# A held output turn, one q chunk and six bank choices moved in a fused attention and SwiGLU kernel

## The chip, the cores and the metric

The kernel runs on one core of a Trainium2 chip. The metric is device time in microseconds (us) of that core, as the median of several executions. The span of a profile, from first to last instruction, is about 1.9 us shorter than the time. Engines are written PE (tensor matmul), PEld (tensor weight load), DVE (vector), ACT (scalar), POOL (GpSimd) and SP (the queue that issues DMAs).

## The reference

```python
# x: 2048 x 640; 32 heads of 192; the last 512 keys and values of the cache; FFN width 1536
def _A_ref(x, k_cache, v_cache, wq, wo):
    W = min(4096, max(256, Sk // 4))                      # 512
    q = (x @ wq).reshape(B, Sq, Hq, Dh).transpose(0, 2, 1, 3)
    k, v = k_cache[:, :, Sk - W:, :], v_cache[:, :, Sk - W:, :]
    p = softmax(einsum("bhqd,bhkd->bhqk", q, k) * Dh ** -0.5)
    o = einsum("bhqk,bhkd->bhqd", p, v)
    return o.transpose(0, 2, 1, 3).reshape(B, Sq, Hq * Dh) @ wo
def _B_ref(x, w_gate, w_up, w_down):
    return (silu(x @ w_gate) * (x @ w_up)) @ w_down
xn = layernorm(x)
return x + _A_ref(xn, ...) * silu(_B_ref(xn, ...))
```

## The kernel before

The FFN comes first (to about 168 us). Then come 16 head pairs. A pair has four blocks of 512 rows; index `i` counts them. In each pair the scores of all four blocks are made, with the q of the next block in three chunks between them. Then the contexts (`pv`) of a block are woven with the output projection (`wo`) of the block two before. PSUM, the memory that PE writes its results to, has two pools of two bank pairs each, `sc` and `mm`; a pair is free again when DVE or ACT has read it. Most matmuls run as two row tiles of 64 rows at once. The kernel lets the two tiles write different banks: context and projection are made in two turns that exchange banks, and a small POOL memset orders the turns. The second turn of a block's last output tile is *held*: it is issued later, inside the next block's contexts or, at the end of a pair, after the next pair's first q chunk.

```python
def sc_tile(): return psum.tile([P, 2, 512], f32, name="sc", tag="sc")     # bufs=2
def mm_tile(): return psum.tile([P, 2, 512], f32, name="mm", tag="mm")     # bufs=2

def q_rows(i, j):                       # one chunk of q: 10 matmuls of 512 columns
    ...
    q_ps = mm_tile()
    for c in range(NC):                 # 5
        for h, r in enumerate((lo, hi)):
            nc.tensor.matmul(q_ps[:, h, :], pairs[pr]["wq"][r, c, ...], xnT[r, c, ...], ...)
    nc.vector.reduce_sum(qTs[i][:, j, :], q_ps[:, :, :].rearrange("p h n -> p n h"), axis=AX.X)

def scores(i, kc):                      # 6 matmuls of 512 columns, then the exponential
    sc = mm_tile() if i == NS - 1 and kc < 2 else sc_tile()
    ...
    nc.scalar.activation(p_t[:, :, :], sc[:, :, :], ACT.Exp, scale=scale)

def pv_full(i, q2):                     # contexts of the last two pairs, full rows
    ...
    acc = sc_tile() if alone and q2 and b < 2 else mm_tile()
    ...                                 # 16 matmuls of 193 columns
    divide(i, q2, acc, alone)           # DVE and ACT into O_b (bufs=2), DMA transpose to OT_b

# wo_tile(i, qt): first() makes turn 0 of an output tile, second() turn 1 and the DVE accumulation
def wo_last(b, qt, eng):                # output tile of the last pair
    ...
    sc = None if split else sc_tile()
    ...
    nc.vector.tensor_tensor(s_f[:], sc[:, :, 0:HD], g2[...], ALU.mult)
    eng.tensor_tensor(ob[:], s_f[...], sacc[:, t, :], ALU.add)   # eng: POOL, for two tiles DVE

held = []
def drop():
    while held:
        held.pop()()

def woven(i):
    (a, b), (w, x, y, z) = (pv(i, 0), pv(i, 1)), (wo_tile(i - 2, qt) for qt in range(4))
    for part in (*a[:2], drop, w[0], *b[:2], w[1], x[0], *a[2:], x[1], y[0], *b[2:], y[1], z[0]):
        part()
    held.append(z[1])                   # the last tile's second turn waits for other work

for pr in range(NPAIR):
    for b in range(NB):
        i = pr * NB + b
        for kc in range(KC):
            if kc < 3 and i + 1 < NS:
                q_rows(i + 1, kc)
                drop()
            scores(i, kc)
            ...
    for b in range(NB):
        i = pr * NB + b
        if i < 2:
            two(pv(i, 0), pv(i, 1))     # both contexts of the block, their turns alternating
        elif pr < last - 1:
            woven(i)
        ...                             # key loads for pair pr + 2 after b == 0
i = last * NB
work = [(0, 0), (0, 1), (1, 0), (1, 1), (2, 0)]
for b, q2 in work:
    pv_full(i + b, q2)
...                                     # then wo_last, woven with the other contexts
```

The softmax here doesn't subtract the row's maximum and nothing guards it: scores larger than these inputs give would overflow.

Of the kernel before, what the change touches and what calls it, by code (L numbers as in the profile page):

```python
# [15 lines left out]
def kernel(  # L16
# [26 lines left out]
    NC = D // P  # L43
    T = Sq // P
    NB = Sq // 512
# [25 lines left out]
    def sc_tile():  # L71
        return psum.tile([P, 2, 512], f32, name="sc", tag="sc")

    def mm_tile():
        return psum.tile([P, 2, 512], f32, name="mm", tag="mm")
# [40 lines left out]
    def load_v(pr):  # L116
        for h in range(2):
            nc.sync.dma_start(
                out=V_p[:, :, h, 0:Dh],
                in_=vv[2 * pr + h, k0:Sk, :].rearrange("(p j) d -> p j d", j=KC),  # L120
            )
# [21 lines left out]
    def sum_k(pr, c):  # L143
        d = pairs[pr]
        nc.vector.reduce_sum(d["ssum"][:, c : c + 1], d["KT"][:, c, :], axis=AX.X)
# [267 lines left out]
    NS = NPAIR * NB  # L413
# [4 lines left out]



    def q_rows(i, j):
        pr, b = divmod(i, NB)
        if j == 0:
            qTs[i] = qpool.tile([P, 3, 512], bf, name="qT")
        q_ps = mm_tile()
        for c in range(NC):
            for h, r in enumerate((lo, hi)):
                nc.tensor.matmul(  # L428
                    q_ps[:, h, :], pairs[pr]["wq"][r, c, j * P : (j + 1) * P], xnT[r, c, b * 512 : (b + 1) * 512],
                    start=(c == 0), stop=(c == NC - 1),  # L430
                )
        with nc.allow_low_precision(reason="a sum of two, rounded once, like a copy out of PSUM"):
            nc.vector.reduce_sum(  # L433
                qTs[i][:, j, :], q_ps[:, :, :].rearrange("p h n -> p n h"), axis=AX.X
            )
# [13 lines left out]
    def pv(i, q2):  # L449

        pr, b = divmod(i, NB)
        st = {}

        def part(p):
            if p == 0:
                if q2 == 0:
                    Obs[i] = opool.tile([P, 4, 2, Dh], bf, name="O_b")
                    tag = "OT_l" if late(i) and pr < last else "OT_b"
                    OTs[i] = otpool.tile([P, 12, P], bf, name=tag, tag=tag, bufs=2 if tag == "OT_l" else 3)
                st["alone"] = i < 2 or (pr == last and 2 * b + q2 < 5)  # L460
                st["acc"] = sc_tile() if st["alone"] and q2 and b < 2 else mm_tile()
            acc = st["acc"]
            turn, h = divmod(p, 2)
            for kc in range(KC):
                for n, r in enumerate((lo, hi)):
                    k = n ^ turn
                    qt = 2 * q2 + k
                    m = nc.tensor.matmul(  # L468
                        acc[:, k, h * 256 : h * 256 + Dh + 1],
                        Ps[i][kc][r, h, qt * P : (qt + 1) * P], V_p[r, kc, h, 0 : Dh + 1],  # L470
                        start=(p == 0 and kc == 0), stop=(turn == 1 and kc == KC - 1),
                        skip_group_check=True,
                    )
                    after(m, st)
            if p == 1:
                turned(m, st)
            if p == 3:
                divide(i, q2, acc, st["alone"])

        return [lambda p=p: part(p) for p in range(4)]  # L480
# [25 lines left out]
    def pv_full(i, q2):  # L506

        pr, b = divmod(i, NB)
        if q2 == 0:
            Obs[i] = opool.tile([P, 4, 2, Dh], bf, name="O_b")  # L510
            tag = "OT_l" if late(i) and pr < last else "OT_b"
            OTs[i] = otpool.tile([P, 12, P], bf, name=tag, tag=tag, bufs=2 if tag == "OT_l" else 3)
        O_b, OT_b = Obs[i], OTs[i]
        alone = i < 2 or (pr == last and 2 * b + q2 < 5)
        acc = sc_tile() if alone and q2 and b < 2 else mm_tile()
        for k in range(2):
            qt = 2 * q2 + k
            for h in range(2):
                for kc in range(KC):
                    nc.tensor.matmul(  # L520
                        acc[:, k, h * 256 : h * 256 + Dh + 1],
                        Ps[i][kc][:, h, qt * P : (qt + 1) * P], V_p[:, kc, h, 0 : Dh + 1],
                        start=(kc == 0), stop=(kc == KC - 1),
                    )
        divide(i, q2, acc, alone)
# [6 lines left out]
    def late(i):  # L532
        return i // NB >= NPAIR - 2 and i % NB >= 2

    def wo_mm(ps, i, qt, n, first=True, end=True):
        for j in range(3):
            nc.tensor.matmul(  # L537
                ps, OTs[i][:, 3 * qt + j, :], pairs[i // NB]["wo"][:, j, n * HD : (n + 1) * HD],
                start=(first and j == 0), stop=(end and j == 2),
            )  # L540
# [8 lines left out]
    def turned(m, st):  # L549

        st["turn"] = nc.gpsimd.memset(turn_t[:], 0.0)  # L551
        follows(st["turn"], m)

    def after(m, st):
        if "turn" in st:
            follows(m, st.pop("turn"))
# [61 lines left out]
    def wo_last(b, qt, eng):  # L618
        i, t = last * NB + b, 4 * b + qt
        ob = xrs[t] if b < 2 else finp.tile([P, D], bf, name="ob", bufs=4)  # L620
        s_f = finp.tile([P, 2, HD], f32, name="s_f", bufs=4)
        halves = [slice(n * HD, (n + 1) * HD) for n in range(2)]
        split = b == NB - 1 and qt == 3
        sc = None if split else sc_tile()
        ps = [(mm_tile()[:, 0, :] if split else sc[:, n, :])[:, 0:HD] for n in range(2)]
        for n, cols in enumerate(halves):
            if late(i):
                wo_mm(ps[n], i - NB, qt, n, end=False)
            wo_mm(ps[n], i, qt, n, first=not late(i))
            if split:  # L630
                nc.vector.tensor_tensor(s_f[:, n, :], ps[n], g2[:, t, cols], ALU.mult)
                nc.vector.tensor_tensor(ob[:, cols], s_f[:, n, :], sacc[:, t, cols], ALU.add)
                (nc.scalar if n else nc.sync).dma_start(
                    out=out2[t * P : (t + 1) * P, cols], in_=ob[:, cols]
                )
        if split:
            return
        nc.vector.tensor_tensor(  # L638
            s_f[:], sc[:, :, 0:HD], g2[:, t, :].rearrange("p (n d) -> p n d", n=2), ALU.mult
        )  # L640
        eng.tensor_tensor(ob[:], s_f[:].rearrange("p n d -> p (n d)"), sacc[:, t, :], ALU.add)
        stores.append((t, ob))
# [4 lines left out]
            nc.sync.dma_start(out=out2[t * P : (t + 1) * P, :], in_=ob[:])  # L647

    held = []

    def two(x, y):
        for part in (*x[:2], *y[:2], *x[2:], *y[2:]):
# [5 lines that stand above are left out]
# [9 lines left out]
    for pr in range(NPAIR):  # L667
        for b in range(NB):
            i = pr * NB + b
            for kc in range(KC):  # L670
                if kc < 3 and i + 1 < NS:
                    q_rows(i + 1, kc)
                    drop()
                scores(i, kc)
                if pr < last:
                    if b == 0:
                        transpose_k(pr + 1, kc)
                    elif b == 2 and kc < 3:
                        sum_k(pr + 1, kc)
                    elif b == 3:  # L680
                        centre_k(pr + 1, kc)
                        if kc == 3:
                            centre_k(pr + 1, 4)
            if b == 0:
                load_v(pr)
                if pr >= last - 1:
                    for t in range(8):
                        load_xr(t + 8 if pr < last else t)
                        if pr == last:
                            add_x(t)  # L690
        if pr == last:
            break
        for b in range(NB):
            i = pr * NB + b
            if i < 2:
                two(pv(i, 0), pv(i, 1))
            elif pr < last - 1:
                woven(i)
            else:
                for q2 in range(2):  # L700
                    pv_full(i, q2)
                    wo_full(i - 2, 2 * q2)
                    wo_full(i - 2, 2 * q2 + 1)
            if b == 0 and pr + 2 < NPAIR:
                load_k(pr + 2)
            elif b == 1 and pr + 2 < NPAIR:
                load_wq(pr + 2)
            elif b == 2:
                load_wo(pr + 1)
    i = last * NB  # L710
    V, G = nc.vector, nc.gpsimd
# [3 lines that stand above are left out]
# [39 lines left out]
```

## Time and profile before

| | before |
|---|---|
| median of the first 3 runs | 927.31 us (926.93 to 928.28) |
| span of the profile | 925.4 us, granted clock 0.999 |
| PE drawn busy | 917.3 us (99%) |
| next engine, DVE | 575.6 us (62%) |

With PE at 99%, the useful question is where it still stands. "Excess" below means how much later a matmul starts than the regular spacing of matmul starts allows, read from the trace; the prediction gives the spacings and shows the lines. The profile's own views show most of the same waits as idle time of PEld.

### The profile page before, as it was taken

Reading aid. Unit: us, or ns where it says so; the run is one execution under the profiler, and the core shown is the slowest. Engines: PE = TensorE matmul, PEld = TensorE weight load, DVE = VectorE, ACT = ScalarE, POOL = GpSimd, SP = SyncE. Lnnn points to the kernel's source line nnn. Section 1 sums busy time; section 2 is a strip of 40 time slices with the busy share of each in tenths; the row PEclk is TensorE's granted clock in tenths of the full one; section 3 lists DMA queues with packets and bytes.
Section 4 is the critical chain, followed back from the end, with each engine's and each line's share of the span. In section 5 each row is a group of like instructions: output and inputs, shape, how many; then the busy total and the mean of one; then the engine's idle time right before and its main releaser. Section 6 shows DMA issues by size and latency. Waiting matters only on the chain.

```text
span 925.4 us, 25770 instructions
## 1 busy us (share of the span) xinstructions
PE 917.3 (99%) x11085; PEld 624.9 (68%) x11101; DVE 575.6 (62%) x844; ACT 473.8 (51%) x847; POOL 100.1 (11%) x387
## 2 busy tenths in 40 slices
PE   9999999999999999999999999999999999999997
PEld 5455556575858585868686867676767777776665
DVE  6433331467676767676766667676767676767655
ACT  4222222556464646565555565656555555556561
POOL 0000000000000000000000000000000000002976
PEclk9999999999999999999999999999999999999999
DMA  9321510044544445444536262536362717162624
GB/s 298 72 56 33 114 35 1 1 77 89 87 79 83 83 80 86 75 90 70 95 60 106 59 107 55 111 53 113 46 119 42 124 36 129 36 129 76 135 57 140
DMA packets 243810, 77.18 MB, mean 83 GB/s; under 512 B 224624, under 2 KB 243696, under 8 KB 243696
## 3 DMA queue, kind: packets, MB, share of 16 engines
q1 hardware_dynamic: 242640, 74.72, 41.5%
q8 instruction: 87, 1.43, 0.7%
q10 hardware_dynamic: 1056, 0.82, 0.3%
q14 instruction: 27, 0.22, 0.1%
HBM read 39.45 MB, written 2.62 MB: 45 GB/s over the span
## 4 chain that ended last, share of the span: by engine, by line
PE 98%; DMA 1%; DVE 0%; issue 0%; ACT 0%; DVEq 0%
PE mm L428 22%; PE sc L563 19%; PE sc L442 18%; PE mm L468 16%; PE sc L276 11%; PE mm L298 6%; PE sc L537 3%; PE mm L520 2%; DMA wg_sb<-in_B_w_gate_dram 1%; PE mm L276 0%; PE mm L311 0%; DMA OT_b<-O_b 0%; PE sc L520 0%; DMA x_t<-in_A_x_dram 0%; DVE s_f L638 0%
## 5 line engine op out<-in xcount | busy, mean ns | idle before, releaser
L446 ACT ACTIVATE p_t<-sc 128x1024 bf16<-128x1024 f32 x254 | 253.0, 1022 | 130.5 <-PE sc L442 130.5
L433 DVE TENSOR_REDUCE qT<-mm 128x512 bf16<-128x1024 f32 x189 | 231.2, 1223 | 104.8 <-PE mm L428 102.4
L498 ACT ACTIVATE O_b<-mm,r 128x192 bf16<-128x192 f32 x486 | 164.6, 421 | 183.1 <-issue 159.9
L428 PE MATMUL mm<-xnT,wq_p 64*128 64x512 bf16 x1890 | 237.7, 377 | 0.0
L563 PE MATMUL sc<-wo_p,OT_b 64*128 64x320 bf16 x2592 | 217.4, 296 | 0.5 <-DMA OT_b<-O_b 0.5
L588 DVE TENSOR_TENSOR sacc<-sacc,sc 128x640 f32<-128x640 f32 x200 | 164.1, 821 | 78.3 <-PE sc L563 78.3
L442 PE MATMUL sc<-qT,khat 64*128 64x512 bf16 x1524 | 198.3, 377 | 0.0
L468 PE MATMUL mm<-V_p,p_t 64*128 64x193 bf16 x3520 | 186.4, 243 | 0.0
L468 PEld LDWEIGHTS <-p_t 64*128 64x128 bf16 x3584 | 162.6, 94 | 12.0
L428 PEld LDWEIGHTS <-wq_p 64*128 64x128 bf16 x1890 | 105.6, 94 | 96.0 <-issue 0.5
L563 PEld LDWEIGHTS <-OT_b 64*128 64x128 bf16 x2592 | 139.9, 94 | 22.7 <-DMA OT_b<-O_b 1.1
L442 PEld LDWEIGHTS <-khat 64*128 64x128 bf16 x1536 | 85.6, 94 | 79.2 <-issue 2.9
L551 POOL MEMSET turn_t<- 128x1 f32 x328 | 32.2, 98 | 697.9 <-PE mm L468 474.6
L284 DVE TENSOR_TENSOR hT<-sc,sg 128x512 bf16<-128x512 f32 x46 | 31.7, 690 | 85.2 <-ACT sg L283 85.1
L283 ACT ACTIVATE sg<-sc 128x512 bf16<-128x512 f32 x46 | 27.3, 596 | 72.4 <-PE sc L276 72.4
L276 PE MATMUL sc<-xnT,wg_sb 128*128 128x512 bf16 (+1 forms) x248 | 58.6, 354 | 1.0 <-DMA wg_sb<-in_B_w_gate_dram 0.4
L276 PE MATMUL sc<-xnT,wu_sb 128*128 128x512 bf16 (+1 forms) x259 | 59.1, 355 | 0.1
L298 PE MATMUL mm<-wd_sb,hT 128*128 128x320 bf16 x384 | 56.6, 300 | 0.0
L487 DVE RECIPROCAL r<-mm 128x4 f32<-128x4 f32 x124 | 22.7, 183 | 48.1 <-PE mm L468 36.3
L298 PEld LDWEIGHTS <-hT 128*128 128x128 bf16 x384 | 37.5, 98 | 18.9
L276 PEld LDWEIGHTS <-wu_sb 128*128 128x128 bf16 x285 | 26.3, 98 | 26.9
L276 PEld LDWEIGHTS <-wg_sb 128*128 128x128 bf16 x285 | 26.3, 98 | 23.5 <-DMA wg_sb<-in_B_w_gate_dram 0.5
(67 smaller groups left out, 373.1 us busy)
## 6 DMA issues: line engine op xcount, KB each, us to landing
wo_p<-in_A_wo_dram SPq DMA_DIRECT2D x16, 480.0 KB, 4.6
K_p<-in_A_k_cache_dram SPq DMA_DIRECT2D x32, 192.0 KB, 3.4
V_p<-in_A_v_cache_dram SPq DMA_DIRECT2D x32, 192.0 KB, 3.0
wq_p<-in_A_wq_dram SPq DMA_DIRECT2D x64, 80.0 KB, 3.1
wq_p<-in_A_wq_dram SPq DMA_DIRECT2D x16, 160.0 KB, 3.5
x_r<-in_A_x_dram SPq DMA_DIRECT2D x16, 160.0 KB, 3.9
x_t<-in_A_x_dram SPq DMA_DIRECT2D x14, 160.0 KB, 3.0
OT_b<-O_b SPq DMA_TRANSPOSE x124, 2.8
```

The costliest lines, as they stand in the source:

```text
L276: nc.tensor.matmul(out, w_sb[:, c, f * P : (f + 1) * P], xnT[:, c, qc], start=(c == 0), stop=(c == NC - 1),)
L284: nc.vector.tensor_tensor(hTs[b][:, f, :], u, sg[:], ALU.mult)
L298: nc.tensor.matmul(dn[:, 0:HD], hTs[b][:, f, ti * P : (ti + 1) * P], wd_sb[:, f, cols], start=(f == 0), stop=(f == NF - 1),)
L428: nc.tensor.matmul(q_ps[:, h, :], pairs[pr]["wq"][r, c, j * P : (j + 1) * P], xnT[r, c, b * 512 : (b + 1) * 512], start=(c == 0), stop=(c ...
L433: nc.vector.reduce_sum(qTs[i][:, j, :], q_ps[:, :, :].rearrange("p h n -> p n h"), axis=AX.X)
L442: nc.tensor.matmul(sc[:, h, :], khat[r, j, ks], qT[r, j, :], start=(j == 0), stop=(j == 2))
L446: nc.scalar.activation(p_t[:, :, :], sc[:, :, :], ACT.Exp, scale=scale)
L468: m = nc.tensor.matmul(acc[:, k, h * 256 : h * 256 + Dh + 1], Ps[i][kc][r, h, qt * P : (qt + 1) * P], V_p[r, kc, h, 0 : Dh + 1], start=(p ...
L498: nc.scalar.activation(O_b[:, qt, h, :], a_k[:, h, 0:Dh], ACT.Copy, scale=r[:, k, h, :])
L551: st["turn"] = nc.gpsimd.memset(turn_t[:], 0.0)
L563: m = nc.tensor.matmul(ps[:, n, 0:HD], OTs[i][r, 3 * qt + j, :], pairs[i // NB]["wo"][r, j, n * HD : (n + 1) * HD], start=(turn == 0 and j ...
L588: nc.vector.tensor_tensor(s_t, s_t, sc[:, :, 0:HD], ALU.add)
```

## The change

The intent was to remove three kinds of waiting. The held turn goes inside the q chunk, so that DVE frees its bank before it reduces the chunk. One q chunk goes where PE waits for the first transposed contexts. In the last pair other banks are used where one was still being read.

```diff
-    def q_rows(i, j):
+    def q_rows(i, j, between=None):
...
         for c in range(NC):
+            if c == NC - 1 and between:
+                between()
...
-        acc = sc_tile() if alone and q2 and b < 2 else mm_tile()        # pv_full
+        acc = sc_tile() if alone and b == 1 else mm_tile()
...
-        sc = None if split else sc_tile()                               # wo_last
+        sc = None if split else mm_tile() if b >= 2 and qt % 2 == 0 else sc_tile()
...
+    EARLY = (NB + 1, 0)
...
-                if kc < 3 and i + 1 < NS:
-                    q_rows(i + 1, kc)
-                    drop()
+                if kc < 3 and i + 1 < NS and (i + 1, kc) != EARLY:
+                    q_rows(i + 1, kc, drop)
...
                 two(pv(i, 0), pv(i, 1))
+                if i == 1:
+                    q_rows(*EARLY)
```

## The prediction

> **What bounds the kernel now.** I read the page's busy table first, then the chain of waits, then what the tensor engine and its weight loads waited for, and last the timeline around each wait. In the table and the chain the tensor engine (PE) is nearly everything:
>
> ```profile
> PE 917.3 (99%) x11085; PEld 624.9 (68%) x11101; DVE 575.6 (62%) x844; ACT 473.8 (51%) x847; POOL 100.1 (11%) x387
> PE 98%; DMA 1%; DVE 0%; issue 0%; ACT 0%; DVEq 0%
> ```
>
> No other engine passes 62%, so the change, which adds no matmul and removes none, can gain only what PE stands still. "99% busy" does not yet say how little that is: a row-tiled matmul of 512 columns is shown 377 ns long while the next pair starts 216 ns after this one, so a stall of up to about 160 ns hides inside the drawn bar. The waits of the weight loads betray them:
>
> ```profile
> PEld L442 <- issue: 2.9, 14, 0.2
> PEld L520 <- issue: 1.1, 3, 0.4
> PEld L563 <- DMA OT_b<-O_b: 1.1, 2, 0.8
> PEld L537 <- issue: 0.4, 1, 0.4
> ```
>
> Fourteen equal waits before the scores (L442), a few elsewhere. I then took every matmul's start in the trace and subtracted the regular spacing (216 ns a pair for 512 columns, 136 for 320, 83 for 193; unpaired matmuls the same). After 168 us, excess over 25 ns is: fourteen times 88 to 99 ns at the second scores tile of a head pair, 1.26 us together; 0.73 and 0.14 us at the first output projections of the first pair, where the transposed context has not landed; 0.26 and 0.33 us in the last pair; and about 0.1 us at each of four switches between row-tiled and full matmuls, which stay. So some 2.7 us of 927 is in reach, all three parts together.
>
> The fourteen, in the timeline of the pair that starts at 256 us:
>
> ```profile
> 256.25 1.26 PE L428 MATMUL mm<-xnT,wq_p 64*128 64x512 bf16 x10
> 257.33 0.59 PE L563 MATMUL sc<-wo_p,OT_b 64*128 64x320 bf16 x6
> 257.55 1.23 DVE L433 TENSOR_REDUCE qT<-mm 128x512 bf16<-128x1024 f32 x1 [0.67 <-PE mm L428]
> 257.74 0.83 PE L442 MATMUL sc<-qT,khat 64*128 64x512 bf16 x6
> 258.69 0.81 DVE L588 TENSOR_TENSOR sacc<-sacc,sc 128x640 f32<-128x640 f32 x1
> 259.56 0.82 PE L442 MATMUL sc<-qT,khat 64*128 64x512 bf16 x6
> ```
>
> To be seen: q chunk (L428), held second turn of the output projection (L563), first scores, then the second scores at 259.56, which need the bank pair that the held turn filled. It is freed by the accumulation L588, ready at about 257.95 but queued behind the 1.23 us reduction of the q chunk. It ends at 259.505; the scores follow 53 ns later, where the spacing would have let them start at 259.468.
>
> **What the Trainium skill says.** (1) "Perfetto Trace Analysis", Summary: the profiler window per engine type: the end of a TensorE instruction is an estimate, that of a DVE or ACT instruction is observed. Hence starts, not busy time; the 377 against 216 ns agrees. (2) "PSUM — Partial Sum Buffer", Engine vs sequencer instructions: the vector and scalar queues are strict FIFO, and matmuls start and complete in program order. The trace agrees: L588 starts only as L433 ends. (3) "TensorEngine Tiling (Array Packing)", Gotcha 1: different row tiles cannot be in one PSUM bank together. That is why a turn exchanges banks through a small memset (L551). It runs 256.56 to 256.66, long before the held turn at 257.33, so bringing that turn 216 ns forward does not meet it.
>
> **The change part by part.** I also read the two built programs' order on each engine with the semaphores waited on; instruction counts are equal, and only places and banks differ.
>
> *Held turn inside the chunk.* The turn now follows four fifths of the q chunk: it starts at 256.255 + 4 x 0.216 = 257.12, issues for 3 x 0.136 = 0.41, and its last matmul ends near 257.71. L588 goes first on DVE, 257.74 to 258.56, and the reduction after it, 258.48 to 259.70. The second scores find their bank free 0.9 us early. The reduction, now later, holds the bank of the third q chunk, which starts near 260.11: 0.35 us margin. Thirteen pairs gain about 90 ns each: -1.17 us. The fourteenth is pair 1, below.
>
> *The q chunk between contexts (first pair).* Before, PE waits for the first transposes:
>
> ```profile
> 197.25 0.73 ACT L498 ACTIVATE O_b<-mm,r 128x192 bf16<-128x192 f32 x2 [1.26 <-DVE r L487]
> 198.22 0.25 PEld L563 LDWEIGHTS <-OT_b 64*128 64x128 bf16 x6 [0.77 <-DMA OT_b<-O_b]
> 198.22 0.58 PE L563 MATMUL sc<-wo_p,OT_b 64*128 64x320 bf16 x6 [0.55 <-DMA OT_b<-O_b]
> ```
>
> Placed at 196.84, the chunk (5 x 0.216 = 1.08 us) fills that hole: the 0.73 goes, and the later 0.14 with it. But it takes one of the two mm bank pairs. The next context waits for the other until ACT ends at 197.98, so it starts at about 198.03 instead of 197.92: +0.11. The one after it takes the chunk's bank: the reduction runs about 198.14 to 199.36, PE could be there at 198.03 + 0.66 + 0.41 = 199.10 and goes at 199.41: +0.31. Net here -0.45 us.
>
> *What its leaving uncovers (pair 1).* The chunk's old place is empty now, and the held turn falls into the next chunk, after the first scores. In the built order the first scores come directly behind the first turn of the last output tile and wait for DVE: their bank is freed by the accumulation of the tile before. Around 209 us that copy is
>
> ```profile
> 208.95 0.82 DVE L586 COPY sacc<-sc 128x640 f32<-128x640 f32 x1 [0.22 <-PE sc L563]
> 209.15 1.24 PE L428 MATMUL mm<-xnT,wq_p 64*128 64x512 bf16 x10
> ```
>
> It ends at 209.77, so PE, which was free for L428 at 209.147, stands until 209.82: +0.68 us. The second scores then get, in the built order, the bank of the first scores and wait for their exponential, not for the held turn: first scores 209.82, exponential 209.82 + 0.85 + 1.02 = 211.69, PE there at 209.82 + 0.65 + 0.86 + 0.41 + 0.22 = 211.96: no wait. The old 0.10 disappears. Net +0.58 us.
>
> *Banks in the last pair.*
>
> ```profile
> 890.08 1.98 ACT L446 ACTIVATE p_t<-sc 128x1024 bf16<-128x1024 f32 x2
> 891.19 0.99 PE L520 MATMUL sc<-V_p,p_t 128*128 128x193 bf16 x10
> 906.50 1.64 DVE L638 TENSOR_TENSOR s_f<-sc,g 128x640 f32<-128x640 f32 x2 [0.70 <-PE sc L537]
> 907.38 0.57 PE L537 MATMUL sc<-wo_p,OT_l 128*128 128x320 bf16 x3 [0.17 <-DVE s_f L638]
> ```
>
> The second context waited for the exponential of the third scores tile (ends 891.10). It now takes the second tile's bank, whose exponential ends at 890.22, before PE comes (890.91): -0.26. The third and fourth take the banks left, free at 891.10 and 892.06 against PE at 892.24 and 893.57. Its own output's transposes still land at 895.72, before PE at 896.26. Likewise the first output tile of the third block takes an mm bank, free since 904.3, instead of waiting at 907.38: -0.33. One new wait appears in the last tile, whose second half needs the bank of the tile before (freed at 919.88, PE there at 919.60), but the end hangs on DVE, which works off its list from 919.06 to 922.60 without pause: nothing. Net -0.60 us.
>
> Sum: -1.17 - 0.45 + 0.58 - 0.60 = -1.64 us. From 927.31 that is 925.7.
>
> **The rivals.** *The moved chunk costs more than it gives.* By my own count it does, +0.13 us for the pair of places, though its purpose was to gain 0.87; if the second scores of pair 1 waited for the held turn as well, that would be 0.85 more, and the time 926.5. The built order speaks against it. *The first scores of pair 1 don't wait*, if DVE gets to the accumulation earlier than I take it: 925.0. The trace has it in every pair at that place, so I don't believe it. *The fourteen waits only move*: the delayed reduction might hold the third chunk's bank. The 0.35 us margin speaks against it; were it so, 926.9. *The last pair is bounded by POOL*, whose additions run without pause from 898.69 to 916.72: then its gain would not reach the end. But DVE's last operations follow PE, not POOL, and POOL would be done 1.3 us ahead still; otherwise 926.3.
>
> **Range and chances.** The three runs before span 926.93 to 928.28, as large as the whole effect, and no stall that I can find exceeds 1 us. I predict 925.7, 924.7 to 927.2 eight times in ten. Two per cent is 18.5 us, seven times all removable waiting: within 2% is all but certain.
>
> **What would show each step.** Held turn: L588 before L433 at each pair's start, no weight-load waits at L442, second scores 216 ns after the last q pair, pairs 47.03 us apart instead of 47.12. Moved chunk: no wait on OT_b near 198 us, but about 0.1 and 0.3 us before the two contexts after it. Pair 1: a single wait of 0.6 to 0.7 us before the first scores, for the copy of L586 (its line moves by two). Last pair: no wait before the second context, nor at the first OT_l tile. I am wrong if pairs 2 to 14 keep a wait before scores or get one before a q chunk, or if the pair-1 wait is missing or above 1 us.

## The result, and the profile after

| | before | after |
|---|---|---|
| median | 927.31 us (3 runs; over 5 runs 926.93 to 928.28) | 925.93 us (5 runs, 925.55 to 926.54) |
| ratio | | 0.9984 (95%: 0.9971 to 0.9998) |
| span of the profile | 925.4 us | 924.2 us |

A ratio is the mean time of one kernel's fast runs over that of the other's of the same rounds, so it is not quite the ratio of the medians. Nothing moved by 2%.

The page after, as bound as before:

```profile
PE 916.6 (99%) x11101; PEld 622.6 (67%) x11101; DVE 576.1 (62%) x844; ACT 473.8 (51%) x847; POOL 100.1 (11%) x387
PE 98%; DMA 1%; DVE 1%; ACTq 0%; issue 0%; ACT 0%; DVEq 0%
```

What the weight loads wait for, without the waits of the FFN (engine, line, releaser: total us, times, longest). The lines of the kernel after are two higher than before, L444 being the scores:

```profile
PEld L522 <- issue: 0.8, 2, 0.4
PEld L444 <- issue: 0.7, 1, 0.7
PEld L470 <- issue: 0.6, 2, 0.3
PEld L430 <- issue: 0.5, 2, 0.3
PEld L539 <- issue: 0.4, 1, 0.4
```

The fourteen waits at the scores are gone; one of 0.7 us stands in their place, and two came at the contexts (L470). The wait at L539 is the new one in the last output tile; its excess is 0.33 us, where the prediction's times give 0.28. The timeline at the same pair as in the prediction (start us, length us, engine, line, operation, count, idle before and releaser):

```profile
256.50 1.04 PE L430 MATMUL mm<-xnT,wq_p 64*128 64x512 bf16 x8
257.37 0.59 PE L565 MATMUL sc<-wo_p,OT_b 64*128 64x320 bf16 x6
257.77 0.40 PE L430 MATMUL mm<-xnT,wq_p 64*128 64x512 bf16 x2
257.99 0.82 DVE L590 TENSOR_TENSOR sacc<-sacc,sc 128x640 f32<-128x640 f32 x1 [0.86 <-PE sc L565]
258.73 2.43 DVE L435 TENSOR_REDUCE qT<-mm 128x512 bf16<-128x1024 f32 x2
259.72 0.83 PE L444 MATMUL sc<-qT,khat 64*128 64x512 bf16 x6
```

The held turn sits between eight and two matmuls of the chunk, the accumulation L590 runs first and ends at 258.81, and the second scores start at 259.72, on spacing. Now the first pair and the start of the second:

```profile
196.93 1.24 PE L430 MATMUL mm<-xnT,wq_p 64*128 64x512 bf16 x10
198.12 0.84 PE L470 MATMUL mm<-V_p,p_t 64*128 64x193 bf16 x16
198.22 1.22 DVE L435 TENSOR_REDUCE qT<-mm 128x512 bf16<-128x1024 f32 x1 [0.29 <-PE mm L430]
198.79 0.58 PE L565 MATMUL sc<-wo_p,OT_b 64*128 64x320 bf16 x6
199.49 0.84 PE L470 MATMUL mm<-V_p,p_t 64*128 64x193 bf16 x16
...
209.68 0.82 DVE L588 COPY sacc<-sc 128x640 f32<-128x640 f32 x1 [0.23 <-PE sc L565]
210.56 0.82 PE L444 MATMUL sc<-qT,khat 64*128 64x512 bf16 x6 [0.51 <-DVE sacc L588]
```

No transpose is waited for, but both contexts start late (excess 0.13 and 0.30 us), the second as the reduction ends at 199.44. The first scores of the second pair start as copy L588 ends (excess 0.69 us).

The last operations of DVE and POOL, first before, then after; L641 and L643 are the additions that make output rows, with both inputs in SBUF, the on-chip working memory:

```profile
913.66 3.05 POOL L641 TENSOR_TENSOR ob<-s_f,sacc 128x640 bf16<-128x640 f32 x2
916.66 0.83 DVE L641 TENSOR_TENSOR ob<-s_f,sacc 128x640 bf16<-128x640 f32 x1
918.33 1.54 POOL L641 TENSOR_TENSOR ob<-s_f,sacc 128x640 bf16<-128x640 f32 x1 [1.62 <-DVE s_f L638]
919.92 0.82 DVE L641 TENSOR_TENSOR ob<-s_f,sacc 128x640 bf16<-128x640 f32 x1
```

```profile
912.74 3.05 POOL L643 TENSOR_TENSOR ob<-s_f,sacc 128x640 bf16<-128x640 f32 x2
915.20 1.27 DVE L643 TENSOR_TENSOR ob<-s_f,sacc 128x640 bf16<-128x640 f32 x1
917.29 1.54 POOL L643 TENSOR_TENSOR ob<-s_f,sacc 128x640 bf16<-128x640 f32 x1 [1.50 <-DVE s_f L640]
918.46 1.05 DVE L643 TENSOR_TENSOR ob<-s_f,sacc 128x640 bf16<-128x640 f32 x1
```

Before, POOL was done (916.71, 919.88) as DVE began. After, DVE begins while POOL still works, and the same DVE additions take 1.27 and 1.05 us instead of 0.83 and 0.82. The prediction did not have this.

The stretches of the span, from matmul starts and DVE ends in the traces. "Block of contexts" means the first context matmul of a pair.

| stretch, us | before | after | moved | predicted |
|---|---|---|---|---|
| first to second block of contexts | 41.442 | 41.600 | +0.16 | +0.13 |
| second to sixteenth block | 656.632 | 655.516 | -1.12 | -1.17 |
| sixteenth block to DVE's last result | 33.022 | 32.657 | -0.37 | -0.60 |
| sum | | | -1.32 | -1.64 |

The start, up to the first row-tiled q chunk, is the same program in all kernels, but took 167.7 to 169.1 us in their fourteen profiles. That is as much as the whole effect; the stretches above are free of it.

### The profile page after: what moved, and what is told of

Its sections match the earlier page's. It is cut to its first block, busy times and chain, and to the rows that moved or that the text cites. A ratio compares the mean times of both kernels' runs of the same rounds, so it can differ in the third digit from the quotient of the medians.

```text
span 924.2 us, 25783 instructions
## 1 busy us (share of the span) xinstructions
PE 916.6 (99%) x11101; PEld 622.6 (67%) x11101; DVE 576.1 (62%) x844; ACT 473.8 (51%) x847; POOL 100.1 (11%) x387
## 4 chain that ended last, share of the span: by engine, by line
PE 98%; DMA 1%; DVE 1%; ACTq 0%; issue 0%; ACT 0%; DVEq 0%
PE mm L430 22%; PE sc L565 19%; PE sc L444 18%; PE mm L470 16%; PE sc L276 11%; PE mm L298 6%; PE sc L539 3%; PE mm L522 2%; PE mm L539 1%; DMA wu_sb<-in_B_w_up_dram 1%; PE mm L276 0%; PE mm L311 0%; PE sc L522 0%; PE sc L470 0%; PE mm L444 0%
## 5 line engine op out<-in xcount | busy, mean ns | idle before, releaser
L590 DVE TENSOR_TENSOR sacc<-sacc,sc 128x640 f32<-128x640 f32 x200 | 164.2, 821 | 89.5 <-PE sc L565 89.5
L444 PE MATMUL sc<-qT,khat 64*128 64x512 bf16 x1524 | 198.1, 376 | 0.5 <-DVE sacc L588 0.5
L470 PE MATMUL mm<-V_p,p_t 64*128 64x193 bf16 x3520 | 186.2, 242 | 0.1
L470 PEld LDWEIGHTS <-p_t 64*128 64x128 bf16 x3584 | 162.4, 93 | 12.9 <-issue 0.6
L444 PEld LDWEIGHTS <-khat 64*128 64x128 bf16 x1536 | 85.1, 94 | 80.1 <-issue 0.7
```

The source lines that it names most:

```text
L444: nc.tensor.matmul(sc[:, h, :], khat[r, j, ks], qT[r, j, :], start=(j == 0), stop=(j == 2))
L470: m = nc.tensor.matmul(acc[:, k, h * 256 : h * 256 + Dh + 1], Ps[i][kc][r, h, qt * P : (qt + 1) * P], V_p[r, kc, h, 0 : Dh + 1], start=(p ...
L590: nc.vector.tensor_tensor(s_t, s_t, sc[:, :, 0:HD], ALU.add)
```

## The experiments

All kernels gave correct results. Each had five timed runs, beside nine of the kernel before on the same chip (medians of before: 927.52 us for the first four, 927.24 for the next four, 927.01 for the next three, 927.05 for the last). The ratios have intervals of about ±0.0013, so differences of a few tenths of a us are read from the stretches of one trace each.

### Each part alone

*Only the held turn.* The change without its other parts:

```diff
-                if kc < 3 and i + 1 < NS and (i + 1, kc) != EARLY:
+                if kc < 3 and i + 1 < NS:
                     q_rows(i + 1, kc, drop)
...
-                if i == 1:
-                    q_rows(*EARLY)
```

(and both bank choices as before)

> Only the held turn moved inside the q chunk. Theory (each part acts through its own wait): all fourteen waits before the second scores vanish, head pairs 47.03 us apart from the second to the fourteenth, nothing else changes, so 14 x 0.086 = 1.2 us faster than the kernel before, near 926.1; the waits for the transposed context (0.73 and 0.14 us) and the two in the last pair (0.26, 0.33) stay. Rival (the gain of the whole change comes mainly from the moved chunk and the banks): pairs stay near 47.12 apart and the time within 0.4 us of before.

Measured: 926.17 us, ratio 0.9985 (0.9972 to 0.9997). Second to sixteenth block 655.52 us, as in the whole change. Its weight loads have no wait at the scores, and still

```profile
PEld L565 <- DMA OT_b<-O_b: 1.2, 2, 0.8
```

In this one trace the second of these waits was 0.23 us instead of 0.14. The held turn alone gives 1.11 us there, of the 1.32 us that the stretches of the whole change add up to.

*Only the chunk.* The kernel before with the chunk taken out at `(i + 1, kc) == EARLY` and called after `i == 1`.

> Only the q chunk brought between the first contexts, everything else as before. Theory: the chunk fills the 0.73 us hole and the later 0.14 goes, but waits of 0.13 and 0.30 us come for the bank pairs, and about 0.69 us before the first scores of the second pair; the time from the first to the second block of contexts grows by about 0.2 us, so the kernel is 0.1 to 0.3 us slower than before, near 927.5. Rival (the chunk pays, as intended): 0.4 to 0.9 us faster.

Measured: 927.74 us, ratio 1.0003 (0.9991 to 1.0016); first to second block 41.689 us against 41.442, excess of 0.13 and 0.30 us at the contexts and 0.69 us at the first scores:

```profile
PEld L442 <- issue: 3.7, 15, 0.7
...
PEld L468 <- issue: 0.6, 2, 0.3
```

Fourteen old waits and the new one. The chunk loses at least what it wins; nothing is seen of the rival's gain.

*Only the contexts' banks*, and *only the late tiles' banks*: the kernel before with one of these lines.

```diff
-        acc = sc_tile() if alone and q2 and b < 2 else mm_tile()
+        acc = sc_tile() if alone and b == 1 else mm_tile()
```

> Only the banks of the last pair's first contexts exchanged; its output tiles as before. Theory: the 0.26 us wait before the second context goes; the tensor engine's last matmul comes 0.26 us sooner; POOL follows only partly (its first addition waits behind a copy that waits for a transpose), so the vector engine's own additions near the end are stretched by up to 0.15 us; end 0.15 to 0.26 us sooner. Rival (POOL plays no part): additions of the vector engine stay at 0.82 to 0.83 us, end 0.26 us sooner.

```diff
-        sc = None if split else sc_tile()
+        sc = None if split else mm_tile() if b >= 2 and qt % 2 == 0 else sc_tile()
```

> Only the banks of the last pair's output tiles exchanged; contexts as before. Theory: the 0.33 us wait before the first late tile goes, one of about 0.3 us appears before the very last half tile without moving the end; POOL's chain of additions is not moved, so the vector engine now overlaps its last additions: its first own addition near the end takes 1.0 to 1.2 us instead of 0.83, the second up to 0.95; end 0.2 to 0.33 us sooner. Rival (no contention): both additions 0.82 to 0.83 us, end 0.33 us sooner.

Measured: 927.08 us (ratio 0.9995) and 926.85 us (0.9994); both intervals include 1. From the sixteenth block to DVE's last result: 32.76 and 32.70 us, thus -0.26 and -0.33. DVE's first addition near the end took 0.98 us in one and 1.05 in the other, the second 0.82 in both, so nothing reached the end. Alone, the two give 0.59 us in sum; together 0.37. The 0.22 us is lost only where both meet, as the stretched additions do.

### Is the end held up by POOL?

*One POOL addition given to DVE*, in the whole change:

```diff
-            wo_last(b, 2 * q2 + k, G)
+            wo_last(b, 2 * q2 + k, V if (b, q2, k) == (1, 1, 1) else G)
```

> The whole change, with one of POOL's twelve last additions (the eighth) given to the vector engine. Theory (the vector engine's own additions are stretched because POOL's additions overlap them): POOL runs about 1 us ahead, no overlap is left near the end, the two additions take 0.82 to 0.83 us instead of 1.27 and 1.05, and the end comes 0.23 us sooner relative to the last matmul. Rival (they are longer because of the other banks or of the stores in flight): they stay above 1.0 us and the end does not move. The given addition itself may take over 1.1 us, off the path.

Measured: 926.32 us, ratio 0.9985; sixteenth block to DVE's last result 32.72 us, no gain. The additions took 1.34 and 1.11 us:

```profile
916.00 1.34 DVE L643 TENSOR_TENSOR ob<-s_f,sacc 128x640 bf16<-128x640 f32 x1
...
919.26 1.11 DVE L643 TENSOR_TENSOR ob<-s_f,sacc 128x640 bf16<-128x640 f32 x1
```

The expectation failed, and the additions and the end are as the rival said; but this does not speak for the rival, since POOL was not relieved. The addition given to DVE ran into POOL's seventh and took 1.96 us, which held up the next product and so POOL's next addition; POOL was as late as before. The misses have a rule, though. In the whole change, this kernel and the two bank kernels, each stretched DVE addition ends 0.68 to 0.69 us after the POOL addition that it met (after: POOL 915.791, DVE 916.472; POOL 918.826, DVE 919.507; here POOL 909.123, DVE 909.809). DVE is not slowed in proportion; it waits until POOL is nearly through.

*A third O_b buffer.* What makes POOL late? In the whole change, the DVE lines before the first product `s_f` are

```profile
895.59 0.18 DVE L489 RECIPROCAL r<-mm 128x4 f32<-128x4 f32 x1 [0.56 <-PE mm L522]
896.33 0.56 DVE L494 TENSOR_TENSOR O_b<-mm,r 128x384 bf16<-128x384 f32 x1 [0.56 <-DMA OT_b<-O_b]
896.81 1.55 DVE L640 TENSOR_TENSOR s_f<-sc,g 128x640 f32<-128x640 f32 x2
```

The copy into `O_b` waits for a transpose to let go of that buffer, the product behind it comes late, and POOL's chain of twelve additions starts from that product.

```diff
-    opool = ctx.enter_context(tc.tile_pool(name="att_o", bufs=2))
+    opool = ctx.enter_context(tc.tile_pool(name="att_o", bufs=3))
```

> The whole change with a third buffer for the contexts before transposing (O_b). Theory (in the last pair a copy of the vector engine waits 0.56 us for a transpose to let go of its buffer, holding up the first product and with it POOL's whole chain of additions, which then overlaps the vector engine's own): the wait goes, POOL starts about 0.45 us sooner relative to the contexts, the first own addition of the vector engine takes 0.82 to 0.86 us and the second 0.82 instead of 1.27 and 1.05, and the time from the last pair's first context to the vector engine's last result falls from 32.66 to about 32.43 us. Rival (the additions are long for another reason): they stay at 1.2 and 1.05, no gain.

Measured: 926.05 us, ratio 0.9986. From the sixteenth block to DVE's last result 32.43 us, as expected; the additions took 0.89 us (a little more than expected; still 0.68 us after POOL's end) and 0.82 us. So POOL's overlap, set by that wait, cost the 0.23 us. The kernel as a whole did not gain, because a new wait of 0.29 us came at 533 us, before a context in the eighth pair.

### Does the chunk pay, and how could it?

*The whole change without the chunk.*

```diff
-                if kc < 3 and i + 1 < NS and (i + 1, kc) != EARLY:
+                if kc < 3 and i + 1 < NS:
...
-                if i == 1:
-                    q_rows(*EARLY)
```

> The whole change without the chunk brought between the first contexts. Theory: the hole of 0.73 us and the 0.14 us wait return, the waits of 0.13, 0.30 and 0.69 us go, and the second pair also gains 0.09 us by the held turn; 0.25 us faster than the whole change, about 1.5 us faster than before. Rival (the chunk pays): slower than the whole change by 0.4 us or more.

Measured: 925.79 us, ratio 0.9982 (0.9968 to 0.9995), against 0.9984 for the whole change in other rounds: not to be told apart. In its profile the first to second block took 41.907 us, *longer* than with the chunk (41.600), against my expectation. The second wait for a transpose was 0.69 us here:

```profile
PEld L565 <- DMA OT_b<-O_b: 1.6, 2, 0.8
```

That wait was 0.14, 0.23, 0, 0 and 0.69 us in the five traces that have neither the chunk nor the key loads moved. I had taken its 0.14 for a constant. With it subtracted, the two kernels that have the held turn but not the chunk come to 41.22 and 41.23 us.

*Without the chunk, keys loaded later.* In the kernel without the chunk, the first pair's load of later keys is issued after the second context's transposes.

```diff
-            if b == 0 and pr + 2 < NPAIR:
+            if b == 0 and 0 < pr and pr + 2 < NPAIR:
                 load_k(pr + 2)
             elif b == 1 and pr + 2 < NPAIR:
+                if pr == 0:
+                    load_k(2)
                 load_wq(pr + 2)
```

> The whole change without the chunk between the contexts, and in the first pair the load of later keys issued after the second context's transposes instead of before them. Theory (the second wait in the first projections, seen at 0 to 0.69 us, is a transpose queued behind that load): the transpose lands about 2.8 us after issue, the second wait is gone and the time from the first to the second block of contexts is 41.21 to 41.23 us, against 41.60 with the chunk: the chunk as built costs 0.38 us there. Rival (the transposes are slow by themselves): landing stays at 3.6 us or more and a wait may remain.

Measured: 925.58 us, ratio 0.9983. First to second block 41.227 us, and only one wait for a transpose is left. What SP issues, without and with this edit:

```profile
197.92 1.22 SPq L101 DMA_DIRECT2D K_p<-in_A_k_cache_dram  x2
199.24 3.60 SPq L503 DMA_TRANSPOSE OT_b<-O_b  x2
```

```profile
195.32 6.11 SPq L503 DMA_TRANSPOSE OT_b<-O_b  x4
201.53 1.23 SPq L101 DMA_DIRECT2D K_p<-in_A_k_cache_dram  x2
```

The transpose is issued 1.2 us sooner and lands at 202.08 instead of 204.62. My reason was only half right: it still takes 4.1 us to land, as the rival said, rather than 2.8; in the other kernels of this stretch it took 3.6 to 5.4. So about half of the 2.5 us is the earlier issue and half a quicker landing (4.1 instead of 5.4 us). PE would have needed the transpose at about 204.1 us, an estimate from the times of the kernel without the chunk; either half alone would have met that, and two of the five traces without this edit had no such wait either. That the earlier issue is what removes the wait is therefore not shown. With the wait absent in this trace, the comparison is clean: the chunk as built costs 41.60 - 41.23 = 0.37 us.

*The second pair's order.* In the whole change, the next chunk, with the held turn in it, goes before the first scores again, and the empty place comes before the second scores.

```diff
+                step = kc
+                if i == NB:
+                    step = {0: 1, 2: 2}.get(kc, 3)
-                if kc < 3 and i + 1 < NS and (i + 1, kc) != EARLY:
-                    q_rows(i + 1, kc, drop)
+                if step < 3 and i + 1 < NS:
+                    q_rows(i + 1, step, drop)
```

> The whole change, but in the second pair the next q chunk (with the held turn in it) goes before the first scores again and the empty place comes after them. Theory (the 0.69 us wait is for the accumulation of the tile before, which has had no time): that wait goes, one of about 0.2 us comes before the second scores, 0.48 us faster than the whole change. Rival (any empty place in this pair costs a whole bank turnover): 0.6 us or more remains.

Measured: 925.57 us, ratio 0.9979 (0.9966 to 0.9991); first to second block 41.141 us, so -0.46. The excess of 0.69 us at the first scores is gone, one of 0.23 us stands at the second. The bank needed only time.

*The chunk in the scores' banks.*

```diff
-                    q_rows(*EARLY)
+                    q_rows(*EARLY, sc=True)      # q_ps = sc_tile() if sc else mm_tile()
```

> The whole change, but the chunk between the contexts is written to the scores' banks instead of the contexts'. Theory (the 0.13 and 0.30 us waits are for banks that the chunk takes out of turn): both go, one of about 0.13 us comes before the first output projection, where the bank of the last context is still being read; 0.3 us faster than the whole change. Rival (the waits come from the chunk's late reduction as such): they stay.

Measured: 926.06 us, ratio 0.9986; first to second block 41.394 us: -0.21, where 0.30 was expected. The 0.13 and 0.30 us at the contexts are gone, 0.14 us came before the first projection, and 0.08 us of the variable wait for a transpose was seen again.

### The best version

*All repairs together:* order, `sc` bank, third `O_b` buffer, keys later.

> The whole change with everything that the runs suggested: chunk in the scores' banks, the second pair's q chunk before its scores again, the third O_b buffer, keys loaded later. Theory: first to second block of contexts 41.60 - 0.46 - 0.30 = about 40.85 us (40.94 if 0.08 of waiting for a transpose stays), last pair 32.43 us; in sum 0.9 to 1.0 us faster than the whole change and 2.2 to 2.4 us faster than before, near 924.9. Rival (the repairs undo each other): gain over the whole change under 0.5 us.

Measured: 925.11 us (924.95 to 925.38), ratio 0.9978 (0.9965 to 0.9990). First to second block 40.860 us, sixteenth block to DVE's last result 32.430: both as expected. Gain over the whole change from the first q chunk to the end: 0.69 us, since the 0.29 us wait, now at 532 us, came again.

*The extra buffer for one context of the last pair only:*

```diff
-            Obs[i] = opool.tile([P, 4, 2, Dh], bf, name="O_b")                    # pv_full
+            own = pr == last and b == 2
+            Obs[i] = opool.tile([P, 4, 2, Dh], bf, name="O_b", tag="O_l" if own else "O_b", bufs=1 if own else 2)
```

> As the combined version, but the extra O_b buffer belongs to one context of the last pair alone, so the buffer rotation of the other pairs stays as in the whole change. Theory (the single new wait of 0.29 us near 532 us, seen with the third buffer in two kernels and in no other, comes with the changed rotation): it is gone, 13 pairs stay 47.03 us apart, first to second block of contexts 40.86 us, last pair 32.43 us; 0.28 us faster than the combined version, 1.2 us faster than the whole change, near 924.8. Rival (that wait was chance): one of this kind may come up again, and the time stays near 925.1.

Measured: 924.82 us (924.71 to 925.63), ratio 0.9975 (0.9962 to 0.9989). No wait at 532 us; second to sixteenth block 655.516, the other stretches as in the version before. The end of its profile:

```profile
913.43 0.82 DVE L641 TENSOR_TENSOR s_f<-mm,g 128x640 f32<-128x640 f32 x1 [0.81 <-PE mm L540]
914.29 0.88 DVE L644 TENSOR_TENSOR ob<-s_f,sacc 128x640 bf16<-128x640 f32 x1
...
917.55 0.82 DVE L644 TENSOR_TENSOR ob<-s_f,sacc 128x640 bf16<-128x640 f32 x1
```

This is the fastest kernel: from the first q chunk to the end 754.93 us in its trace, against 755.89 for the whole change and 757.23 before. Why the three-buffer rotation waited at that one place stays open. In the whole change too, a reciprocal of DVE comes 0.35 us later there (531.09 us) than at the same place of the pairs around, without consequence; what delays it is not shown.

## Why the prediction was right, and what it missed

The time was predicted as 925.7 us and measured as 925.93, within the range; "within 2%" held. The time alone tests little: its interval allows a gain of 0.2 to 2.7 us, so that the medians agree to 0.2 us is partly luck, and the steps have to be judged by the stretches. By its steps:

- **Held turn: right.** Accumulation before reduction, pairs 47.03 us apart instead of 47.12 (both as predicted), 13 times 0.086 us where 0.09 was said. The experiment with it alone shows that this is its work alone.
- **The q chunk between contexts: right in its waits, incomplete in the reference.** Predicted +0.11 and +0.31, measured 0.13 and 0.30 us. The 0.14 us that was to disappear is not a constant: it was 0 to 0.69 us over five traces without the chunk.
- **What its leaving uncovers: right.** 0.68 us predicted, 0.69 measured, released by copy L588. The second scores did not wait, as the built order said. The changed order shows the cause: with other work in front the wait goes.
- **Banks in the last pair: the mis-sized term.** -0.60 was predicted, -0.37 measured. PE did gain it: the last matmul before the split tile started 0.59 us sooner after the pair's first context. The step that failed reads "the end hangs on DVE, which works off its list from 919.06 to 922.60 without pause: nothing", together with the rival on POOL, dismissed with "POOL would be done 1.3 us ahead still". I asked whether POOL's *results* would be late. They were not. I did not ask whether DVE and POOL would now *work at the same time*. Counted from the pair's first context, PE and DVE moved forward by 0.59 us, POOL's last chained addition by 0.05, since a transpose held up the chain's first input; the overlap of 0.05 us before became 0.59 us, and DVE's additions waited for POOL. The buffer that moved POOL forward gave the 0.23 us back.

The Trainium skill would have told: "SBUF — State Buffer", Who interferes with whom, says that "a DVE instruction with two SBUF inputs contends with a GpSimd instruction that reads SBUF", and that one with at most one SBUF input, outside the two-port modes, doesn't. The traces agree with both: the addition of two SBUF tiles was stretched to between 0.88 and 1.96 us where it overlapped POOL by 0.20 us or more (overlaps of up to 0.14 us, as of the second addition with the tile banks alone, left it at 0.82 us), while the product `s_f`, which reads one operand from PSUM, stayed at 0.82 us under POOL's additions (before, 909.28 us).

The sum of the stretches in the traces is -1.32 us, and the medians differ by 1.38; the predicted -1.64 is off by 0.23 us at the end and by 0.08 in two smaller terms (0.03 and 0.05).

## What to carry to other kernels

When an engine is 99% busy, list the excess over its regular start-to-start spacing; here that gave waits that the drawn bars hide, and three new ones were predicted to about 0.02 us (the fourth, off the path, to 0.05). Before moving work into a hole, look at what the work hid in its old place, and which buffer it takes out of turn in the new one: the moved chunk filled a hole of 0.73 us and uncovered waits of 1.1 us. And when a faster chain meets an engine that stays behind, check which operations will newly overlap, not only who is done first.

## What the Trainium skill lacked or had wrong

- "SBUF — State Buffer", Who interferes with whom: right in which DVE operations meet POOL. Its section "SBUF: two separate sides" says that whichever starts first holds the shared ports for the whole instruction and the other "fully blocks". POOL began first in every stretched case here, and a DVE addition that takes 0.82 us alone ended 0.68 to 0.69 us after POOL's recorded end: 1.27 us long with 0.59 us of overlap, 1.05 with 0.37, and 1.96 when it began 0.26 us after POOL. That is a block, not a slowdown, but one that costs about 0.14 us less than the whole overlap (0.82 - 0.68). The page gives no such figure for two SBUF inputs; recorded spans of POOL are rough.
- "Perfetto Trace Analysis", Optimization Strategy: advises to look for gaps between an engine's slices. The fourteen waits of 90 ns left no gap on PE, whose slices of 377 ns overlap at a spacing of 216 ns. They showed as idle time of the weight loads (2.9 us in 14 waits) and in the starts. The same page calls matmul busy time a bad metric for this engine (99% drawn busy before and after); what it lacks is how to find such waits.
- "DMA: Bandwidth & Descriptors", Latency and other measured facts: gives a bandwidth for DMA transposes, but no time to landing. Between two tiles in SBUF the median was 2.8 us over the 128 transposes of the contexts in the kernel before, with a quarter of them at 4.0 to 5.5 us; one around 200 us took 3.6 to 5.4 us over the kernels.
- No page that I read warns that moving one tile changes which bank every later tile gets. In the built order, the second scores of the second pair thus needed a bank that ACT frees instead of one that DVE frees, and they did not wait; the prediction, from the trace of before, estimates that the other bank would have cost 0.85 us. No run tried it.
